# Splitting the last value load and cast of batch 0, making x by halves, and putting a piece of a cast ahead of the weight loads

## The chip, the cores and the metric

The kernel runs on one core of a Trainium2 chip. The metric is the device time of one execution in microseconds (us); less is better. A profile's own clock counts from the first instruction of the program to the last. That length is called the span and is 1.9 to 2.2 us shorter than the device time in the profiled runs here. Engines: PE is the matmul engine, PEld its weight loads, DVE the vector engine, ACT the scalar engine, POOL is GpSimd, SP issues most DMAs.

## The reference

Efficient attention for 8 batches of 8 heads (576 positions, head width 64), then a SwiGLU block over all 4608 tokens:

```python
q_s = softmax(q, axis=-1); k_s = softmax(k, axis=2)          # per head
kv  = einsum('bhsd,bhse->bhde', k_s, v)
x   = einsum('bhsd,bhde->bhse', q_s, kv)                     # tokens x 512
out = (silu(x @ w_gate) * (x @ w_val)) @ w_out               # 512 -> 1536 -> 512
```

## The kernel before

The eight heads make two groups of four, G = 0 and 1. A group's x needs its q (exp, row sums, multiply to `qs`, transpose to `qt`), its k (exp) and its v (cast to bf16). `kv` is K^T V with a column of ones beside V, whose result scales `kv` to `kn`. The block then runs in chunks of tokens: batch 0 is the first chunk (576 tokens). All is issued in a fixed order per engine. The parts that the change touches:

```python
WARM = (64, 8, 8)                         # dummy matmuls, to bring PE to its full clock
def load(b, G, what, src, after=None):    # one DMA on SP's queue, 576 KB
    raw[what, b, G] = ld.tile([128, 2, T * 64], FP32, ...)
    ...
def x(b, G, piece, eng=nc.scalar):        # four 64x64 matmuls side by side
    xp = [f_tile("xp") for _ in range(2)]
    for g in range(2):
        for h in range(2):
            r = slice(64 * h, 64 * h + 64)
            matmul(out=xp[h][64*g:64*g+64, ...], lhsT=kn[r, g, :], rhs=qt[g][r, t0:t1, :])
    ...                                   # xp[0] copied by ACT, xp[1] by DVE
# ---- the start
load q(0,0), q(0,1); for G in 0, 1: load k(0,G), v(0,G)
exp q, norms: qs of group 0 on POOL, of group 1 on DVE
exp(0, 0, "k"); cast_v(0, 0, nc.scalar)
# weights on POOL's queue, fp32 in HBM, cast to bf16 by the DMA, held back until v(0,0) landed
for c0, n in ((0, 256), (256, 256), (512, 512), (1024, 512)): wg slice, wv slice
wo slices (three)
warm_up(WARM[0]); transposes; exp k(0,1); kv(0,0); kn
cast_v(0, 1, nc.vector, *A); cast_v(0, 1, nc.scalar, *Z)     # tiles 0-4 and 5-8
warm_up(WARM[1]); x(0,0,A); x(0,0,Z); kv(0,1); kn
warm_up(WARM[2]); x(0,1,A); x(0,1,Z)
load(1, 0, "q", q, after=w_dma[-3])       # batch 1: after the first wo slice has landed
...
for m in range(12): m_unit(0, S, m)       # g_ps, u_ps: gate and value matmuls of chunk 1
```

The softmax here doesn't subtract the row's maximum and nothing guards it: scores larger than these inputs give would overflow.

Of the kernel before, what the change touches and what calls it, by code (L numbers as in the profile page):

```python
# [8 lines left out]
FP32 = mybir.dt.float32  # L9
# [6 lines left out]
def kernel(  # L16
# [19 lines left out]
    nc = tc.nc  # L36

    B, H, S, D = q.shape
# [4 lines left out]
    T = S // 64  # L43
    HSTR = S * D
    NG = H // 4
    RING = 1536
    WARM = (64, 8, 8)

    const = ctx.enter_context(tc.tile_pool(name="const", bufs=1))
    ld = ctx.enter_context(tc.tile_pool(name="ld", bufs=3))  # L50
# [5 lines left out]
    def f_tile(name):  # L56
        return psp.tile([128, 512], FP32, tag="ps", name=name)
# [4 lines left out]
    xt = const.tile([128, KT, n_tok], BF16, name="xt", tag="xt")  # L62
# [4 lines left out]
    dmas = {}  # L67
    raw = {}

    def load(b, G, what, src, after=None):  # L70
        raw[what, b, G] = ld.tile([128, 2, T * 64], FP32, tag=what, name=what)
        ap = bass.AP(
            tensor=src.tensor,
            offset=src[b, 4 * G].offset,
            ap=[[T * 64, 128], [2 * HSTR, 2], [1, T * 64]],
        )
        d = nc.sync.dma_start(out=raw[what, b, G], in_=ap)  # L77
        if after is not None:
            tc.add_manual_dep(d.ins, after.ins.name, SYNC, reason="order of loads")
        dmas[what, b, G] = d  # L80
# [21 lines left out]
    def copy(eng, out, in_):  # L102
        if eng is nc.scalar:
            nc.scalar.copy(out=out, in_=in_)  # L104
        else:
            eng.tensor_copy(out=out, in_=in_)  # L106


    st = {}
    BANKS = ((0, 5), (5, 9))  # L110

    def exp(b, G, what):
        s = st.setdefault((b, G), {"vb": vbs[G]})
# [7 lines left out]
    def cast_v(b, G, eng, t0=0, t1=T):  # L121
        copy(
            eng,
            vbs[G][:, t0:t1, 0:128].rearrange("p t (h d) -> p t h d", d=64),
            raw["v", b, G].rearrange("p h (t d) -> p t h d", d=64)[:, t0:t1],
        )
# [19 lines left out]
    def norm(b, G):  # L146
        norm_sum(b, G)
        norm_mul(b, G, nc.vector)
# [46 lines left out]
        for g in (1, 0):  # L195
            nc.vector.reciprocal(out=s["kvr"][:, g:g + 1], in_=s["kv"][g][:, 128:129])

    def kn(b, G, g, eng):
        s = st[b, G]
        if "kn" not in s:  # L200
            s["kn"] = at.tile([128, 2, 64], BF16, tag="kn", name="kn")
        for h in range(2):
            r = slice(64 * h, 64 * h + 64)
            out_, src, sc = s["kn"][r, g, :], s["kv"][g][r, r], s["kvr"][r, g:g + 1]
            if eng is nc.scalar:
                nc.scalar.mul(out_, src, sc)
            else:
                nc.vector.tensor_scalar_mul(out_, src, sc)  # L208

    def x(b, G, piece, eng=nc.scalar):  # L210
        s = st[b, G]
        t0, t1 = piece
        n = 64 * (t1 - t0)
# [4 lines that stand above are left out]
                nc.tensor.matmul(  # L218
                    out=xp[h][64 * g:64 * g + 64, 0:n].rearrange("p (t c) -> p t c", c=64),
                    lhsT=s["kn"][r, g, :],  # L220
                    rhs=s["qt"][g][r, t0:t1, :],
                    start=True, stop=True,
                )
        c0 = b * S + 64 * t0
        copy(eng, xt[:, 2 * G, c0:c0 + n], xp[0][:, 0:n])
        nc.vector.tensor_copy(out=xt[:, 2 * G + 1, c0:c0 + n], in_=xp[1][:, 0:n])  # L226

    def x_both(b, G, eng=nc.scalar):
        for piece in BANKS:
            x(b, G, piece, eng)  # L230
        st.pop((b, G))
# [92 lines left out]


    make_identity(nc, ident)
    A, Z = BANKS
    with tc.manual_schedule():
        for G in range(NG):
            load(0, G, "q", q)  # L330
        for G in range(NG):
            load(0, G, "k", k)
            load(0, G, "v", v)
        warm = const.tile([128, 1], FP32, name="warm", tag="warm")
        nc.vector.memset(warm, 0.0)
        nc.scalar.activation(out=warm, in_=warm, func=AF.Exp)
        zero = const.tile([128, 256], BF16, name="zero", tag="zero")
        nc.vector.memset(zero, 0.0)  # L338
        for vb in vbs:
            nc.vector.memset(vb[:, :, 128:129], 1.0)  # L340

        exp(0, 0, "q")
        exp(0, 1, "q")
        norm_sum(0, 0)
        norm_mul(0, 0, nc.gpsimd)
        norm_sum(0, 1)
        norm_mul(0, 1, nc.vector)
        exp(0, 0, "k")
        cast_v(0, 0, nc.scalar)

        w_dma = []
        for c0, n in ((0, 256), (256, 256), (512, 512), (1024, 512)):
            w_dma.append(w_slice(wg, moe_w_gate, c0, n))
            w_dma.append(w_slice(wv, moe_w_val, c0, n))
        tc.add_manual_dep(w_dma[0].ins, dmas["v", 0, 0].ins.name, SYNC, reason="order of loads")
        for m0 in (0, 4, 8):
            w_dma.append(wo_slice(m0, 4))

        warm_up(WARM[0])
        for G in range(NG):  # L360
            for piece in BANKS:
                tr(0, G, piece, nc.vector)
        exp(0, 1, "k")
        kv(0, 0)
        kn_recip(0, 0)
        kn(0, 0, 1, nc.scalar)
        kn(0, 0, 0, nc.vector)
        cast_v(0, 1, nc.vector, *A)
        cast_v(0, 1, nc.scalar, *Z)
        warm_up(WARM[1])  # L370
        x(0, 0, A)
        x(0, 0, Z)
        kv(0, 1)
        kn_recip(0, 1)
        kn(0, 1, 1, nc.scalar)
        kn(0, 1, 0, nc.vector)
        warm_up(WARM[2])
        x(0, 1, A)
        x(0, 1, Z)

        load(1, 0, "q", q, after=w_dma[-3])
        load(1, 1, "q", q)
        for G in range(NG):
            load(1, G, "k", k)
            load(1, G, "v", v)
        load_group(2, 0)

        for m in range(MT):
            m_unit(0, S, m)

        exp(1, 0, "q")
        exp(1, 1, "q")
        exp(1, 0, "k")
        cast_v(1, 0, nc.gpsimd)
        cast_v(1, 1, nc.gpsimd)
        load_group(2, 1)
        o_unit(0, nc.scalar)
        norm(1, 0)
        o_unit(1, nc.scalar)
        exp(1, 1, "k")  # L400
        norm(1, 1)
        o_unit(2, nc.scalar)
        for piece in BANKS:
            tr(1, 0, piece, nc.vector)
        kv_kn(1, 0, split=True)
        for piece in BANKS:
            tr(1, 1, piece, nc.vector)
        exp(2, 0, "q")

        def between():  # L410
            kv_kn(1, 1, split=True)
            x_both(1, 0, nc.vector)

        finish = o_unit(3, between=between)
        exp(2, 0, "k")
        x_both(1, 1)
        finish()
        norm(2, 0)
        tr_dma(2, 0)
        cast_v(2, 0, nc.gpsimd)  # L420
        cast_v(2, 1, nc.gpsimd)
        exp(2, 1, "q")
        exp(2, 1, "k")

        chunks = [(S, 448)] + [(c, 512) for c in range(1024, n_tok, 512)]
        for ci, (c0, n) in enumerate(chunks):
            b = ci + 2
            first_o = 4 * ci
            final = ci == len(chunks) - 1
            steps = {}  # L430
            if ci == 0:
                steps = {2: lambda: kv_kn(2, 0, True), 4: lambda: x_both(2, 0),
                         7: lambda: kv_kn(2, 1, True), 10: lambda: x_both(2, 1)}
            elif b < B:
                steps = {8: lambda: kv_pair(b), 9: lambda: x_both(b, 0),
                         10: lambda: x_both(b, 1)}
            for m in range(MT):
                if ci == 0 and m == 4:
                    norm_sum(2, 1)
                    norm_mul(2, 1, nc.gpsimd)  # L440
                    tr_dma(2, 1)
                    load_group(3, 0)
                    load_group(3, 1)
                if ci > 0 and m in (3, 7):
                    if b < B:
                        att_head(b, m // 4)
                        if m == 7 and b + 1 < B:
                            load_group(b + 1, 0)
                            load_group(b + 1, 1)
                    o_unit(first_o + (0 if m == 3 else 2))  # L450
                    if not (final and m == 7):
                        o_unit(first_o + (1 if m == 3 else 3))
                m_unit(c0, n, m)
                if m in steps:
                    steps[m]()
        o_unit(first_o + 3)
        last = n_tok // 128 - 4
        for j in range(last, last + 3):
            o_unit(j)
        o_last(last + 3)  # L460
# [30 lines left out]
```

## Time and profile before

Median 319.42 us of the first three runs.

| what | at, us | view |
|---|---|---|
| first v of batch 0 lands, weights begin to be issued | 9.68, 9.99 | timeline, DMA landings |
| second v lands | 12.64 | DMA landings |
| first block matmul (g_ps) | 15.68 | timeline of PE |
| third wv load lands, PE waits 0.33 for it | 24.77 | waits of PEld |
| q of batch 1 issued, lands | 33.23, 40.04 | chain of waits |
| second chunk's first matmul | 53.55 | timeline of PE |

The page first: busy time by engine, then (of its picture in 40 slices, 7.9 us each) the tenths in which PE and the DMA engines are busy.

```profile
PE 310.4 (98%) x1920; PEld 157.1 (50%) x1948; DVE 175.5 (55%) x332; ACT 149.2 (47%) x224; POOL 31.1 (10%) x33
...
PE   8999999999999999999999999999999999999995
...
DMA  7999999449145905392519440963150213020134
```

PE is nearly never idle, but in the first six or seven slices the DMA engines are full too. So two resources run abreast at the start. The timeline of POOL before the change (start us, length us, then engine, line, operation, out<-in and, in brackets, idle time before and what ended it):

```profile
7.29 2.12 POOL L140 TENSOR_TENSOR qs<-eq,rr 128x1152 bf16<-128x1152 bf16 x1 [5.99 <-DVE rr L135]
9.99 0.93 POOL L92 DMA_DIRECT2D wg<-in_moe_w_gate_dram  x1 [0.57 <-DMA v<-in_v_dram]
```

The weights start when v has landed. The chain of work that ended last, in order of time, cut to the start of the kernel:

```profile
2.26 7.42 DMA v<-in_v_dram
9.99 0.93 POOL wg L92
16.05 17.16 DMA wo<-in_moe_w_out_dram
33.23 6.82 DMA q<-in_q_dram
40.11 1.28 ACT L115
```

Read it as: v, then the issue of the weights, then a wo load (issued at 16.05, landed at 33.21, behind all weights ahead of it), then q of batch 1, then ACT. In this execution the chain doesn't go through the x of batch 0 at all. PE's timeline and its waits for weights:

```profile
15.26 0.49 PE L218 MATMUL xp<-qt,kn 64*64 64x320 bf16 x8
15.68 1.26 PE L270 MATMUL g_ps<-xt,wg 128*128 128x320 bf16 x8
```
```profile
PEld L270 <- DMA wv<-in_moe_w_val_dram: 0.3, 1, 0.3
```

DVE around the casts:

```profile
9.37 1.36 DVE L140 TENSOR_TENSOR qs<-eq,rr 128x1152 bf16<-128x1152 bf16 x1
...
13.03 0.56 DVE L106 CAST vb<-v 128x640 bf16<-128x640 f32 x1
```
```profile
313.87 0.29 DVE L322 COPY o_sb<-o_ps 128x128 f32<-128x128 f32 x1 [0.38 <-PE o_ps L318]
```

Last, two casts of the same shape on POOL, later in the kernel, of which the first was started during a qs multiply on DVE (44.35 to 45.71):

```profile
44.68 2.03 POOL L106 CAST vb<-v 128x1152 bf16<-128x1152 f32 x1 [25.26 <-ACT ek L115]
...
52.20 1.15 POOL L106 CAST vb<-v 128x1152 bf16<-128x1152 f32 x1 [2.52 <-DMA v<-in_v_dram]
```

### The profile page before, as it was taken

What the parts mean: (1) busy time and instruction counts of PE and PEld (TensorE: products, weight loads), DVE (VectorE), ACT (ScalarE), POOL (GpSimd) and SP (SyncE); (2) the same over time, 40 slices, a digit from 0 to 9 for tenths busy, and PEclk for the clock granted to TensorE, in tenths of its full rate; (3) what the DMA queues carried; (4) which work ended last, traced back from release to release, by engine and by line L of the source; (5) the groups of instructions that cost most, each with busy time, mean ns of one, the idle gap of its engine ahead of it and who ended that gap; (6) DMA issues with size and microseconds to landing.
All of it is one profiled execution on the core that took longest, in us unless ns stands there. A gap on an engine that the chain in (4) does not pass through costs nothing.

```text
span 317.4 us, 5037 instructions
## 1 busy us (share of the span) xinstructions
PE 310.4 (98%) x1920; PEld 157.1 (50%) x1948; DVE 175.5 (55%) x332; ACT 149.2 (47%) x224; POOL 31.1 (10%) x33
## 2 busy tenths in 40 slices
PE   8999999999999999999999999999999999999995
PEld 6777744554445444444444444444444444444444
DVE  2934479964647664774577366746575333333422
ACT  4753387744763475547364547355734122312300
POOL 1930023121100110011001100020000000000000
PEclk9999999999999999999999999999999999999999
DMA  7999999449145905392519440963150213020134
GB/s 269 252 190 206 281 392 393 130 116 367 22 84 153 379 24 103 74 385 94 103 38 355 162 103 1 310 241 64 41 103 2 44 22 67 3 61 5 35 67 99
DMA packets 39176, 46.34 MB, mean 146 GB/s; under 512 B 16368, under 2 KB 22384, under 8 KB 39152
## 3 DMA queue, kind: packets, MB, share of 16 engines
q1 hardware_dynamic: 33104, 41.17, 42.5%
q0 software_dynamic: 5808, 4.72, 9.7%
q8 instruction: 15, 0.25, 0.3%
q10 hardware_dynamic: 240, 0.13, 0.2%
q14 instruction: 9, 0.07, 0.1%
HBM read 37.75 MB, written 9.44 MB: 149 GB/s over the span
## 4 chain that ended last, share of the span: by engine, by line
PE 82%; DMA 10%; DVE 3%; POOL 2%; ACT 1%; issue 1%; SPq 0%; DVEq 0%; ACTq 0%
PE g_ps L270 26%; PE o_ps L297 26%; PE u_ps L270 26%; DMA wo<-in_moe_w_out_dram 5%; PE kv L184 2%; DMA v<-in_v_dram 2%; DMA q<-in_q_dram 2%; PE xp L218 1%; POOL wg L92 1%; POOL wv L92 1%; DVE qs L140 1%; PE o_ps L318 1%; DVE rs L131 1%; DVE xt L226 0%; SPq L77 0%
## 5 line engine op out<-in xcount | busy, mean ns | idle before, releaser
L278 ACT ACTIVATE sg<-g_ps 128x512 bf16<-128x512 f32 (+2 forms) x120 | 64.9, 554 | 132.9 <-PE g_ps L270 126.8
L279 DVE TENSOR_TENSOR hr<-sg,u_ps 128x512 bf16<-128x512 bf16 (+2 forms) x120 | 74.9, 633 | 90.7 <-PE u_ps L270 84.1
L270 PE MATMUL g_ps<-xt,wg 128*128 128x512 bf16 (+2 forms) x469 | 110.3, 358 | 0.7
L270 PE MATMUL u_ps<-xt,wv 128*128 128x512 bf16 (+2 forms) x468 | 109.6, 357 | 0.7
L297 PE MATMUL o_ps<-wo,hr 128*128 128x512 bf16 x415 | 93.3, 379 | 0.3
L270 PEld LDWEIGHTS <-wv 128*128 128x128 bf16 x480 | 46.9, 98 | 46.9 <-issue 0.3
L270 PEld LDWEIGHTS <-wg 128*128 128x128 bf16 x480 | 45.3, 98 | 46.2 <-issue 2.6
L297 PEld LDWEIGHTS <-hr 128*128 128x128 bf16 x420 | 41.0, 98 | 49.1 <-issue 0.2
L106 POOL CAST vb<-v 128x1152 bf16<-128x1152 f32 x14 | 17.8, 1270 | 167.2 <-DMA v<-in_v_dram 115.0
L131 DVE TENSOR_REDUCE rs<-eq 128x18 f32<-128x1152 bf16 x16 | 21.6, 1352 | 21.9 <-ACT eq L115 21.8
L106 DVE COPY o_sb<-o_ps 128x512 f32<-128x512 f32 x32 | 21.1, 686 | 20.6 <-PE o_ps L297 20.6
L140 DVE TENSOR_TENSOR qs<-eq,rr 128x1152 bf16<-128x1152 bf16 x14 | 19.8, 1415 | 0.5
L115 ACT ACTIVATE eq<-q 128x1152 bf16<-128x1152 f32 x16 | 18.5, 1163 | 3.2 <-DMA q<-in_q_dram 3.1
L115 ACT ACTIVATE ek<-k 128x1152 bf16<-128x1152 f32 x16 | 18.4, 1152 | 1.3 <-DMA k<-in_k_dram 1.3
L278 ACT ACT_TABLE_LOAD x12 | 15.4, 1283 | 0.2
L208 DVE TENSOR_SCALAR kn<-kv,kvr 64x64 bf16<-64x64 f32 x52 | 14.7, 283 | 1.3
L115 ACT ACT_TABLE_LOAD x11 | 14.1, 1283 | 0.9 <-DMA q<-in_q_dram 0.7
L104 ACT CAST xt<-xp 128x320 bf16<-128x320 f32 (+1 forms) x30 | 10.5, 402 | 6.6 <-PE xp L218 6.6
L226 DVE CAST xt<-xp 128x320 bf16<-128x320 f32 (+1 forms) x32 | 13.1, 450 | 0.5 <-PE xp L218 0.5
L249 PE MATMUL warm_ps<-zero 128*128 128x256 bf16 x80 | 10.9, 302 | 1.1 <-DVE zero L338 1.1
L184 PE MATMUL kv<-vb,ek 64*128 64x129 bf16 x288 | 10.3, 218 | 0.2 <-DVE vb L106 0.2
L184 PEld LDWEIGHTS <-ek 64*128 64x128 bf16 x288 | 8.4, 94 | 3.9 <-ACT sg L278 2.1
(32 smaller groups left out, 64.5 us busy)
## 6 DMA issues: line engine op xcount, KB each, us to landing
q<-in_q_dram SPq DMA_DIRECT2D x16, 576.0 KB, 7.0
k<-in_k_dram SPq DMA_DIRECT2D x16, 576.0 KB, 8.5
v<-in_v_dram SPq DMA_DIRECT2D x16, 576.0 KB, 9.4
out_dram<-o_sb SPq DMA_DIRECT2D x70, 128.0 KB, 2.4
wo<-in_moe_w_out_dram POOLq DMA_DIRECT2D x3, 512.0 KB, 19.0
wg<-in_moe_w_gate_dram POOLq DMA_DIRECT2D x2, 512.0 KB, 11.3
wv<-in_moe_w_val_dram POOLq DMA_DIRECT2D x2, 512.0 KB, 13.1
wg<-in_moe_w_gate_dram POOLq DMA_DIRECT2D x2, 256.0 KB, 6.0
```

The costliest lines, as they stand in the source:

```text
L106: eng.tensor_copy(out=out, in_=in_)
L115: nc.scalar.activation(out=s["e" + what], in_=raw[what, b, G].rearrange("p h (t d) -> p t h d", d=64), func=AF.Exp,)
L131: nc.vector.reduce_sum(out=rs, in_=s["eq"].rearrange("p t h d -> p (t h) d"), axis=mybir.AxisListType.X)
L140: eng.tensor_mul(s["qs"].rearrange("p t (h d) -> p (t h) d", d=64), s["eq"].rearrange("p t h d -> p (t h) d"), s["rr"].to_broadcast([128, ...
L184: nc.tensor.matmul(out=s["kv"][g][:, 0:129], lhsT=s["ek"][r, t, :, :].rearrange("p h d -> p (h d)"), rhs=s["vb"][r, t, 0:129], start=(t == 0),
L208: nc.vector.tensor_scalar_mul(out_, src, sc)
L226: nc.vector.tensor_copy(out=xt[:, 2 * G + 1, c0:c0 + n], in_=xp[1][:, 0:n])
L249: nc.tensor.matmul(out=ps[:, 0:256], lhsT=zero[:, 0:128], rhs=zero, start=True, stop=True)
L270: nc.tensor.matmul(out=p_[:, 0:w_], lhsT=w[:, kk, ms], rhs=xt[:, kk, c:c + w_], start=(kk == 0), stop=(kk == KT - 1),)
L278: nc.scalar.activation(out=sg[:, 0:w_], in_=g_ps[:, 0:w_], func=AF.Silu)
L279: nc.vector.tensor_mul(hr[:, m, r:r + w_], sg[:, 0:w_], u_ps[:, 0:w_])
L297: nc.tensor.matmul(out=o_ps, lhsT=hr[:, m, r0:r0 + 128], rhs=wo[:, m, :], start=(m == 0), stop=(m == MT - 1),)
```

## The change

Its intent is to have the second x of batch 0 sooner, so that the first chunk starts sooner: the second v in two loads, its cast in three pieces, kn and x by half (h = 0, then h = 1) so that the first half's matmuls need only half of kn, fewer dummies in between. A small piece of the first v's cast goes to POOL, and so the weights are issued a little later and leave the queue to the second v.

```diff
-    WARM = (64, 8, 8)
+    WARM = (64, 6, 5)
...
-        for G in range(NG):
-            load(0, G, "k", k)
-            load(0, G, "v", v)
+        load(0, 0, "k", k)
+        load(0, 0, "v", v)
+        load(0, 1, "k", k)
+        load(0, 1, "v", v, None, *A)          # tiles 0-4
+        load(0, 1, "v", v, None, *Z)          # tiles 5-8
...
-        cast_v(0, 0, nc.scalar)
+        cast_v(0, 0, nc.scalar, 0, 7)
+        cast_v(0, 0, nc.gpsimd, 7, 9)         # POOL, ahead of the weights' issue
...
         cast_v(0, 1, nc.vector, *A)
-        cast_v(0, 1, nc.scalar, *Z)
+        cast_v(0, 1, nc.scalar, 5, 7)
+        cast_v(0, 1, nc.vector, 7, 9)
...
-        kn(0, 1, 1, nc.scalar)
-        kn(0, 1, 0, nc.vector)
+        for h in range(2):
+            kn(0, 1, 1, nc.scalar, h, h + 1)
+            kn(0, 1, 0, nc.vector, h, h + 1)
         warm_up(WARM[2])
-        x(0, 1, A)
-        x(0, 1, Z)
+        x_by_half(0, 1)                       # per h, per piece: two matmuls (g = 0, 1), one copy
```

More of the change, by code (lines that the diff above doesn't have):

```diff
@@ L68, with load @@
     raw = {}
-    def load(b, G, what, src, after=None):
-        raw[what, b, G] = ld.tile([128, 2, T * 64], FP32, tag=what, name=what)
+    def load(b, G, what, src, after=None, t0=0, t1=T):
+        if (what, b, G) not in raw:
+            raw[what, b, G] = ld.tile([128, 2, T * 64], FP32, tag=what, name=what)
         ap = bass.AP(
             tensor=src.tensor,
-            offset=src[b, 4 * G].offset,
-            ap=[[T * 64, 128], [2 * HSTR, 2], [1, T * 64]],
+            offset=src[b, 4 * G].offset + 64 * t0,
+            ap=[[T * 64, 128], [2 * HSTR, 2], [1, (t1 - t0) * 64]],
         )
-        d = nc.sync.dma_start(out=raw[what, b, G], in_=ap)
+        d = nc.sync.dma_start(out=raw[what, b, G][:, :, t0 * 64:t1 * 64], in_=ap)
         if after is not None:
@@ L109 @@
     st = {}
-    BANKS = ((0, 5), (5, 9))
+    A, Z = BANKS = ((0, 5), (5, 9))
     def exp(b, G, what):
@@ L196, in kn_recip, with kn @@
             nc.vector.reciprocal(out=s["kvr"][:, g:g + 1], in_=s["kv"][g][:, 128:129])
-    def kn(b, G, g, eng):
+    def kn(b, G, g, eng, h0=0, h1=2):
         s = st[b, G]
@@ L201, in kn @@
             s["kn"] = at.tile([128, 2, 64], BF16, tag="kn", name="kn")
-        for h in range(2):
+        for h in range(h0, h1):
             r = slice(64 * h, 64 * h + 64)
@@ L226, in x, with x_by_half @@
         nc.vector.tensor_copy(out=xt[:, 2 * G + 1, c0:c0 + n], in_=xp[1][:, 0:n])
+    def x_by_half(b, G):
+        s = st[b, G]
+        for h, eng in ((0, nc.scalar), (1, nc.vector)):
+            r = slice(64 * h, 64 * h + 64)
+            for t0, t1 in BANKS:
+                n = 64 * (t1 - t0)
+                xp = f_tile("xp")
+                for g in range(2):
+                    nc.tensor.matmul(
+                        out=xp[64 * g:64 * g + 64, 0:n].rearrange("p (t c) -> p t c", c=64),
+                        lhsT=s["kn"][r, g, :],
+                        rhs=s["qt"][g][r, t0:t1, :],
+                        start=True, stop=True,
+                    )
+                c0 = b * S + 64 * t0
+                copy(eng, xt[:, 2 * G + h, c0:c0 + n], xp[:, 0:n])
     def x_both(b, G, eng=nc.scalar):
@@ L326 @@
     make_identity(nc, ident)
-    A, Z = BANKS
     with tc.manual_schedule():
```

## The prediction

> **What bounds the kernel.** The page: PE busy 98% of 317.4 us, so only idle or dummy PE time can be won. The timeline: real FFN matmuls begin at 15.68 us and then have almost no gap. The front is bound by a second thing, the DMA queues, full from 2.5 to 47.5 us (the page's DMA digits). Landings in the trace: first v of batch 0 at 9.68, second v 12.64; then the weights in order of issue: wg 15.18, wv 16.37, 18.39, 19.69, wg 22.22, wv 24.77, 28.18, 30.66, wo 33.21. Only then is q of batch 1 issued; it lands at 40.04, just when ACT wants it. PE already waits for this chain: the fifth u_ps group starts at 24.81 after 0.33 us for a wv load; and the chain of waits runs wo load, q load, table load, exp, two norms on DVE, transposes at 48.73, x, g_ps at 54.6.
>
> So x(0,1) being ready earlier gains nothing alone: PE would wait longer at 24.8 and 48.7. What counts is when the weights land.
>
> **What the change does.**
> 1. x by half: the first pair of kn (0.3 us each) releases the first matmuls, about 0.3 us less before x. But DVE gets one more cast, of 128x256 (estimate 0.25 us, from 0.56 for 128x640), ahead of its xt copies. Together about 0. The second v landed at 12.64 but its casts began at 13.01, behind kn, so landing earlier is hardly used.
> 2. Five dummy matmuls fewer: 5 x 0.12 us, not on the chain.
> 3. A 128x256 cast on POOL goes ahead of the weights' issue (before: 9.99). DVE's qs multiply runs 9.37 to 10.73. The Trainium skill, "SBUF — State Buffer", section "Who interferes with whom", says that a DVE instruction with two SBUF inputs and a GpSimd one that reads SBUF block each other for a whole instruction. The trace agrees: a POOL cast alone took 1.15 us (at 52.2), but 2.03 and 1.99 when started during a qs multiply, ending 1.00 after it both times. So the cast should wait to 10.73 and end near 10.95 (2/9 of 1.0), and the first weight issue move to about 11.0. The queue was partly filled with v until 12.1, so I estimate that weights land about 0.5 us later (82 KB moved before the new start, at 160 GB/s). If the cast isn't blocked, 0.1 to 0.2.
>
> **Sum.** x about where it was (15.3), g_ps 15.7 to 15.9, perhaps a short new wait for the first wv; the fifth u_ps group starts near 25.3; q of batch 1 lands near 40.5; all the rest shifts by 0.3 to 0.5 us. Nothing else changes after 55 us, nor the PE clock.
>
> Predicted: 319.7 us, 8 in 10 between 318.7 and 320.7. Faster by over 2%: 0.005; within 2%: 0.985; slower by over 2%: 0.01.
>
> **What would show it.** POOL's small cast ends after DVE's qs multiply; first wg issue near 11.0; third wv landing after 25.0; a longer wait of u_ps on wv; q of batch 1 later than 40.1. Wrong if the first wg issue comes before 10.4, or the weights land no later.
>
> **What would make it wrong.** The weights, no longer sharing the queue with v, may land as early as before; then the time is the same to 0.2 us. Or fewer bubbles in their stream (110 GB/s at 15 to 16 us, otherwise 160) give up to 0.5 us of gain. Fewer dummies could drop the PE clock; I don't expect it.

## More of the kernel before

```profile
SPq L486 <- DMA out_dram<-o_sb: 0.7, 3, 0.3
```

The end of the kernel (last copy of the result; who SP waited for after it): from the end of that last copy (314.17) to the end of the span (317.37) there are 3.20 us. I call this stretch the tail; the prediction did not look at it.

## The result, and the profile after

The changed kernel took 320.8 us (median of six runs, 319.96 to 321.56), beside 319.35. The ratio is 1.0044 with a 95% interval of 1.0023 to 1.0065. Ratios here are the mean time of one kernel's fast runs over that of the other's of the same rounds, so not quite the ratio of the medians. In two later jobs of six runs each the changed kernel had 1.0021 and 1.0035. It is slower by 0.2 to 0.45%, about 1.06 us on average (means of 1.39, 0.72 and 1.08 us). The forecast was 0.3 us, with 320.7 us as the upper end of its range.

The profile of the changed kernel. POOL, whose cast now stands between qs and the weights:

```profile
7.31 2.12 POOL L141 TENSOR_TENSOR qs<-eq,rr 128x1152 bf16<-128x1152 bf16 x1 [6.00 <-DVE rr L136]
9.41 1.49 POOL L107 CAST vb<-v 128x256 bf16<-128x256 f32 x1
10.85 0.93 POOL L93 DMA_DIRECT2D wg<-in_moe_w_gate_dram  x1
```

DVE: its qs multiply, and its two casts of the second v in one row:

```profile
8.70 1.94 DVE L141 TENSOR_TENSOR qs<-eq,rr 128x1152 bf16<-128x1152 bf16 x1
...
12.95 1.16 DVE L107 CAST vb<-v 128x640 bf16<-128x640 f32 x2
```

The multiply ended at 10.64 and the POOL cast 0.25 us after it, so a cast of 256 columns took 1.49 us. PE, and its waits:

```profile
15.47 0.75 PE L237 MATMUL xp<-qt,kn 64*64 64x320 bf16 x8 [0.36 <-DVE kn L209]
16.15 1.15 PE L288 MATMUL g_ps<-xt,wg 128*128 128x320 bf16 x8
...
26.69 1.15 PE L288 MATMUL u_ps<-xt,wv 128*128 128x320 bf16 x8 [0.98 <-DMA wv<-in_moe_w_val_dram]
```
```profile
PEld L288 <- DMA wv<-in_moe_w_val_dram: 1.8, 2, 1.3
```

The wait for the third wv grew from 0.33 to about a microsecond on PE. The chain of waits after, again cut to its start:

```profile
7.31 2.12 POOL qs L141
9.43 1.47 POOL vb L107
10.90 0.88 POOL wg L93
14.70 11.94 DMA wv<-in_moe_w_val_dram
26.69 1.15 PE u_ps L288 x8
```

The small POOL cast, the issues of weights and the third wv load are now the chain, and from 26.69 on it stays with PE; q of batch 1 is no longer on it. And the end of the kernel:

```profile
315.53 0.29 DVE L340 COPY o_sb<-o_ps 128x128 f32<-128x128 f32 x1 [0.38 <-PE o_ps L336]
```
```profile
SPq L507 <- DMA out_dram<-o_sb: 1.3, 1, 1.3
```

Here the tail (315.82 to 319.44) is 3.62 us, and SP's waits for the stores look different: one of 1.3 us in place of three of at most 0.3.

A DMA is done when all of its 16 shares, one from each DMA engine, have landed. The times of the 16 for the third wv load, read from its semaphore's updates in the two traces:

```
before  23.39 23.89 23.96 24.12 24.13 24.19 24.20 24.21 24.26 24.29 24.35 24.36 24.44 24.47 24.63 24.77
after   24.09 24.11 24.14 24.26 24.33 24.34 24.36 24.38 24.41 24.45 24.46 24.55 24.61 24.81 25.68 26.64
```

The middle of the load is 0.2 us later than before, the last share 1.9 us. This agrees with what the Trainium skill, "DMA: Bandwidth & Descriptors", section "Why a DMA increments its semaphore by 16 and not by 1", says: the engines finish independently, and only the full count means that all has landed. The forecast reckoned with a load as a whole.

### The profile page after: what moved, and what is told of

Read it like the earlier page. It is cut to its first block, busy times and chain, and to the rows that moved or that the text cites. A ratio compares the mean times of both kernels' runs of the same rounds, so it can differ in the third digit from the quotient of the medians.

```text
span 319.4 us, 5059 instructions
## 1 busy us (share of the span) xinstructions
PE 312.2 (98%) x1943; PEld 156.6 (49%) x1943; DVE 175.7 (55%) x333; ACT 149.1 (47%) x224; POOL 33.0 (10%) x34
## 4 chain that ended last, share of the span: by engine, by line
PE 89%; DMA 5%; POOL 2%; DVE 2%; ACT 0%; issue 0%; POOLq 0%
PE g_ps L288 28%; PE u_ps L288 28%; PE o_ps L315 28%; DMA wv<-in_moe_w_val_dram 4%; PE kv L185 3%; PE xp L219 1%; DMA q<-in_q_dram 1%; PE o_ps L336 1%; POOL wg L93 1%; POOL qs L141 1%; POOL wv L93 0%; POOL vb L107 0%; DVE xt L227 0%; DVE rs L132 0%; ACT eq L116 0%; PE tp L161 0%
## 5 line engine op out<-in xcount | busy, mean ns | idle before, releaser
L288 PE MATMUL u_ps<-xt,wv 128*128 128x512 bf16 (+2 forms) x480 | 111.0, 358 | 1.2 <-DMA wv<-in_moe_w_val_dram 1.2
L288 PE MATMUL g_ps<-xt,wg 128*128 128x512 bf16 (+2 forms) x480 | 111.6, 358 | 0.2
L107 POOL CAST vb<-v 128x1152 bf16<-128x1152 f32 (+1 forms) x15 | 19.8, 1317 | 166.7 <-DMA v<-in_v_dram 114.5
L227 DVE CAST xt<-xp 128x320 bf16<-128x320 f32 (+1 forms) x30 | 12.2, 448 | 0.0
```

What stands on the lines that cost most here:

```text
L107: eng.tensor_copy(out=out, in_=in_)
L227: nc.vector.tensor_copy(out=xt[:, 2 * G + 1, c0:c0 + n], in_=xp[1][:, 0:n])
L288: nc.tensor.matmul(out=p_[:, 0:w_], lhsT=w[:, kk, ms], rhs=xt[:, kk, c:c + w_], start=(kk == 0), stop=(kk == KT - 1),)
```

## The experiments

There were five jobs; within a job all kernels share one chip and the runs of the kernel before. The names: a_ is the changed kernel with something taken back, b_ is the kernel before with one thing done. All results were correct; one execution was slow, and is told of. What the traces showed, in us; the last columns are explained below the table:

| kernel | ratio (95% interval) | first wg issued | third wv landed | q of batch 1 landed | first g_ps | chunk 2 begins | tail |
|---|---|---|---|---|---|---|---|
| before | 1 | 9.99 | 24.77 | 40.04 | 15.68 | 53.55 | 3.20 |
| after | 1.0044 (1.0023, 1.0065) | 10.85 | 26.64 | 41.19 | 16.15 | 55.21 | 3.62 |
| after_again | 1.0021 (1.0006, 1.0036) | 10.94 | 24.51 | 39.94 | 16.25 | 53.59 | 3.62 |
| after_third | 1.0035 (1.0020, 1.0049) | 10.94 | 25.98 | 40.53 | 16.26 | 54.55 | 3.64 |
| a_nopool | 1.0006 (0.9993, 1.0018) | 10.23 | 24.63 | 39.55 | 17.04 | 54.44 | 3.65 |
| b_pool | 1.0009 (0.9998, 1.0021) | 10.87 | 25.40 | 40.70 | 16.51 | 54.20 | 3.19 |
| b_pool_again | 1.0014 (0.9998, 1.0029) | 11.05 | 25.84 | 40.83 | 16.68 | 54.42 | 3.21 |
| b_split | 1.0010 (0.9996, 1.0023) | 10.37 | 25.25 | 40.73 | 16.75 | 54.24 | 3.63 |
| b_tiny1 | 1.0005 (0.9993, 1.0018) | 9.52 | 24.19 | 38.93 | 15.90 | 53.36 | 3.62 |
| a_tiny7 | 1.0025 (1.0012, 1.0039) | 10.93 | 26.09 | 40.47 | 16.25 | 54.66 | 3.20 |
| b_warm54 | 1.0002 (0.9990, 1.0015) | 10.11 | 25.25 | 39.79 | 15.74 | 53.82 | 3.19 |
| b_qearly | 1.0021 (1.0006, 1.0036) | 10.53 | 25.47 | 37.96 | 16.16 | 55.33 | 3.22 |
| b_delay2 | 1.0075 (1.0046, 1.0104) | 12.01 | 26.69 | 41.10 | 16.14 | 57.00 | 3.19 |
| b_xhalf | 1.0004 (0.9991, 1.0017) | 10.36 | 25.30 | 39.63 | 15.99 | 53.86 | 3.20 |
| b_early | 1.0003 (0.9989, 1.0016) | 9.58 | 25.47 | 40.58 | 15.95 | 54.08 | 3.21 |
| best2 | 0.9991 (0.9977, 1.0005) | 9.48 | 24.30 | 39.34 | 15.85 | 53.30 | 3.23 |
| best2_again | 0.9994 (0.9978, 1.0009) | 9.41 | 24.10 | 38.52 | 15.93 | 53.77 | 3.20 |
| a_fix (fast runs) | 0.9989 (0.9976, 1.0003) | slow | slow | slow | slow | slow | slow |
| a_fix_again | 1.0002 (0.9990, 1.0014) | 9.43 | 24.36 | 38.67 | 16.23 | 53.58 | 3.19 |
| best3 | 1.0007 (0.9992, 1.0021) | 9.37 | 24.30 | 38.81 | 16.18 | 54.26 | 3.21 |

"Chunk 2 begins" is the first matmul of the second chunk. Between it and the end of the last copy of the result there are 260.6 to 260.7 us in every fast trace: span = beginning of chunk 2 + 260.6 + tail. So all that the change can do is in two numbers, and the rest of the kernel is a constant. One trace is one execution, and executions of one kernel differ by several tenths; the ratios rest on five or six runs (eleven of before in the later jobs).

### Is the late share a matter of chance? (after_again, after_third: no edit)

> The changed kernel once more, unchanged. In its first trace 14 of the 16 shares of the third wv load had landed by 24.8 us, but the last two at 25.7 and 26.6, and PE waited 0.98 us for the last. Theory S (a late share is a matter of chance in each execution): the late shares are elsewhere or smaller in this trace, the wait of u_ps on the third wv is under 0.6 us, and the time of this execution is near 320. Theory P (it belongs to the change): again two late shares, third wv whole after 26 us. Time: 1.003 to 1.006 of before.

> The changed kernel unchanged, for the size of its loss: 1.002 to 1.0045. Weights issued at 10.9 us once more, third wv whole between 24.5 and 26.7 us, tail 3.6 us.

In after_again the third wv was whole at 24.51 and its last two shares 0.01 us apart; PE did not wait for it. In after_third the last share came 0.75 us after the one before, and PE waited 0.78 us. So the size of the lag is different in each execution. It is not the change's alone either: in b_early (below) one share came 1.5 us after the other fifteen. What makes a DMA engine fall behind stays open; the packed traces don't say which engine a share came from. The issue of the weights, however, was at 10.85 to 10.94 in all four traces with the whole change's POOL piece (a_tiny7 is the fourth).

after_again shows one thing more. The chain of waits that ended last has no load of weights or of batch 1 there. It goes through DVE's casts of the second v and x of batch 0 (at 15.56) to the first g_ps; two of its lines:

```profile
13.33 0.87 DVE vb L107 x2
16.32 1.09 PE g_ps L288 x8
```

Chunk 2 begins 37.34 us after the first g_ps there (16.25 to 53.59), with no wait of PE over 0.25 us between. In nine of the 19 fast traces the chain goes through x in this way: after_again, a_nopool, b_pool_again, b_split, b_tiny1, best2, best2_again, a_fix_again and best3. In the other ten it comes from a late load. So there are two limits, and the later one counts.

### One part taken out, or done alone (a_nopool, b_pool, b_pool_again, b_split)

a_nopool, out of the changed kernel, and b_pool the reverse, into the kernel before:

```diff
-        cast_v(0, 0, nc.scalar, 0, 7)
-        cast_v(0, 0, nc.gpsimd, 7, 9)
+        cast_v(0, 0, nc.scalar)
```

b_split is the kernel before with the second v in two loads, as in the change's diff, and nothing else.

> The changed kernel with the first v cast whole on ACT, as before, so that the weights are issued right after v lands. Theory 1 (the POOL piece, held up by the qs multiply, delays the weights, and all else follows): first weight issue back at about 9.9 us, third wv whole by 25.0, time within 0.1% of before (ratio 0.999 to 1.001). Theory 2 (the split load of the second v, with its smaller packets, or the DVE casts, make the weights late): still 1.003 or more. Theory 3 (x comes later): g_ps still starts near 16.1 us, and the time is 1.001 to 1.002.

> The kernel before with one part of the change alone: the last two ninths of the first v cast on POOL ahead of the weights' issue. Theory 1: cast ends right after the qs multiply, first weight issue at 10.8 us, third wv later than 25 us, ratio 1.003 to 1.005, all of the change's loss. Theories 2 and 3: ratio under 1.002.

> The kernel before with the second v of batch 0 in two loads and nothing else. Theory 1: ratio 0.999 to 1.001. Theory 2 (the two loads leave some of the 16 DMA engines behind, and the weights behind them): late shares of the weights, ratio 1.002 or more.

> The kernel before with the POOL piece alone, once more: first weight issue at 10.9 us, tail 3.2 us, ratio 1.0005 to 1.002; about the changed kernel's ratio less 0.0013 for the tail.

POOL in b_pool, and in a_nopool:

```profile
9.70 1.22 POOL L106 CAST vb<-v 128x256 bf16<-128x256 f32 x1 [0.25 <-DMA v<-in_v_dram]
10.87 0.93 POOL L92 DMA_DIRECT2D wg<-in_moe_w_gate_dram  x1
```
```profile
10.23 0.94 POOL L93 DMA_DIRECT2D wg<-in_moe_w_gate_dram  x1 [0.71 <-DMA v<-in_v_dram]
```

DVE's multiply ended at 10.66 in b_pool, the cast at 10.92: held up again. But neither single part had the whole loss, as my theory 1 wanted. b_pool's mean was 0.36 and 0.47 us over before, a_nopool's 0.36, b_split's 0.36. All four intervals hold 1, so the sizes are rough; a_nopool against the changed kernel in the same job is 0.37 us less. The trace of a_nopool has its own delay: PE's full clock came late (6.98 us), g_ps began at 17.04, and chunk 2 began 37.4 us after that. Theory 1 alone falls: something else is in a_nopool and in b_split, and the traces say where. Their tail is 3.65 and 3.63 us, as in all traces with the split load, and 3.2 in all without.

### The tail (b_tiny1, a_tiny7)

DMAs of SP and ACT take eight semaphores (the counters by which a DMA tells that it has landed) in turn. At the end of the program SP waits for each semaphore, one after the other, in a fixed order. The second v in two loads is one DMA more, so from there on every DMA has the next semaphore. SP's last waits, by the time each was over, read from the traces, with the landing of the last store:

```
before  315.22 315.29 315.36 315.42 315.48 315.64 315.86 316.23 316.52                    last store lands 316.47
after   316.86 318.16 318.23 318.29 318.35 318.41 318.47 318.53 318.59                    last store lands 318.12
```

Before, the last store had the semaphore that is waited for last, so the other waits were done by the time it landed. After, it has one that is waited for second: SP stands there until 318.12, and only then goes through the seven others, at about 0.06 us each. That is the 0.42 us. To test it, small DMAs that nobody reads, in the middle of the kernel (one into the kernel before, seven into the changed kernel):

```diff
+                if ci == 3 and m == 9:
+                    scr = const.tile([128, 8], FP32, name="scr", tag="scr")
+                    for e in range(1):        # a_tiny7: range(7)
+                        nc.sync.dma_start(out=scr[:, e:e + 1], in_=<one column of q>)
                 m_unit(c0, n, m)
```

> The kernel before with one further DMA of 512 bytes in the middle (about 150 us), read by nobody. Theory T (tail): in four traces with the second v in two loads, the time from the last copy of the result to the end is 0.41 us longer than in the two traces without, because the count of DMAs on the eight semaphores shifts by one, the last store falls on the semaphore that SP waits for second to first at the end, and seven waits of about 0.06 us follow it instead of one. So this kernel too has a tail 0.4 us longer (3.6 us from the last copy's end to the end of the span, not 3.2), and a ratio near 1.0013. If the tail comes of the split load itself, the tail is as before.

> The changed kernel with seven such DMAs of 512 bytes in the middle, so that the count is 8 more than before and the last store has its old semaphore again. Theory T: the tail is back to 3.2 us, and the time is 0.4 us below the changed kernel's: ratio 1.0005 to 1.001 where the changed kernel had 1.002. Rival: the tail stays at 3.6 us, and the ratio at 1.002 or more.

The ends of b_tiny1 (span 317.6) and of a_tiny7 (span 318.5), last copy and SP's waits:

```profile
313.67 0.29 DVE L322 COPY o_sb<-o_ps 128x128 f32<-128x128 f32 x1 [0.38 <-PE o_ps L318]
```
```profile
SPq L494 <- DMA out_dram<-o_sb: 1.2, 1, 1.2
```
```profile
314.99 0.29 DVE L340 COPY o_sb<-o_ps 128x128 f32<-128x128 f32 x1 [0.38 <-PE o_ps L336]
```
```profile
SPq L515 <- DMA out_dram<-o_sb: 0.8, 3, 0.3
```

One DMA of 512 bytes, at 172.8 us in this trace, makes the tail 3.62 us, and seven bring the changed kernel's back to 3.20. The cause of the longer tail is settled: it is the place of the last store among the eight semaphores (one DMA more than before, or eight more), not the split load as such. The times are not as clear: b_tiny1 had 1.0005, not 1.0013, and a_tiny7 1.0025, no less than after_again in another job. Its trace shows why: the third wv landed at 26.09 and PE waited 0.65 us for it. The spread of the loads hides 0.4 us in six runs; the tail in the traces does not vary by more than 0.05.

### Do the landings hang on the issue? (b_delay2)

```diff
+        pad = const.tile([128, 2304], FP32, name="pad", tag="pad")
+        d = nc.gpsimd.memset(pad, 0.0)        # waits for v(0,0), ahead of the weights
```

> The kernel before with a memset of an unused 128x2304 tile on POOL ahead of the weights' issue, waiting for the same v [...]. Theory D (loads of the weights hang on their issue one to one, and the time on their landing): first weight issue near 12 us, third wv lands near 26.8 us, q of batch 1 near 42 us, PE waits over 1 us for the third wv, ratio 1.005 to 1.007. If the landings are set by the queue and not by the issue, they move by under 1 us and the ratio stays under 1.003.

The issue moved by 2.02 us (9.99 to 12.01) and the third wv by 1.92 (24.77 to 26.69), but q of batch 1 only by 1.06 (40.04 to 41.10, not to 42). One trace is little to go by. A straight line through the 20 traces (one of them slow) gives 0.89 us of landing of the third wv for each us of issue (standard error 0.15), and 0.86 for q of batch 1 (0.23). So landings follow the issue nearly one to one on average. The time grew by 2.4 us on average, but not by the landings alone. What I hadn't foreseen is in PE's timeline and in the busy time of stretches of this trace (columns: stretch, length, busy us and count of PE, PEld, DVE, ACT, POOL, granted PE clock, DMA share, GB/s):

```profile
18.97 2.10 PE L270 MATMUL u_ps<-xt,wv 128*128 128x320 bf16 x8 [1.68 <-DMA wv<-in_moe_w_val_dram]
20.87 1.91 PE L270 MATMUL g_ps<-xt,wg 128*128 128x320 bf16 x8
22.61 1.14 PE L270 MATMUL u_ps<-xt,wv 128*128 128x320 bf16 x8
```
```profile
15.00:19.00 4.00, 2.01 (x21) 1.04 (x20) 1.13 (x4) 3.00 (x6) 4.00 (x6) 1.00 1.36 178
19.00:22.40 3.40, 3.40 (x15) 2.15 (x16) 0.82 (x2) 0.00 (x0) 1.51 (x3) 0.50 1.29 197
```

After an idle time of 1.68 us PE's clock was halved for 3.4 us, and eight matmuls took 2.10 us, not 1.14. Three of the six runs had a mean clock of 0.992 to 0.995 and took 322.8 to 323.5 us; the three with 0.999 to 1.0 took 320.5 to 321.4, which is 1.3 us over before on average. So at full clock the 2.0 us of delay cost 1.3 us, and the runs with the lower clock took another 2.2: waiting for a load can be paid twice. In the changed kernel the clock didn't fall so (0.997 to 1.0).

### x by half (b_xhalf)

> The kernel before with x of the second group by half, kn by head, and three dummy matmuls fewer just before it; no split load, no new cast. In the traces of the changed kernel x begins about 0.3 us after the first kn, but its eight matmuls then take 0.69 us to the first g_ps rather than 0.42, since a half has only two matmuls that run side by side where the old form has four. Theory X: x begins 0.2 to 0.3 us sooner and g_ps no sooner than before (15.6 to 15.9 us after an early clock), ratio 0.9995 to 1.0005. The intent of the change would give g_ps 0.3 us sooner.

In the kernel before with kn and x by half (with WARM (64, 8, 5)), x and the first g_ps began as follows:

```profile
15.30 0.76 PE L236 MATMUL xp<-qt,kn 64*64 64x320 bf16 x8
15.99 1.15 PE L287 MATMUL g_ps<-xt,wg 128*128 128x320 bf16 x8
```

From x to g_ps there are 0.69 us, where before there were 0.42. The old form starts four 64x64 matmuls within 0.06 us of each other, on four quarters of the array (in the trace of before at 15.257, 15.312, 15.316 and 15.319); by half it is two at a time, and four such pairs take their turns. x itself began at 15.30, before at 15.26, but in this execution the second v had landed 0.37 us later (13.01, before 12.64), and kn began 0.31 us later (14.90, before 14.59). Against kn, then, x began 0.27 us sooner, as expected. What the halved kn wins, x by half gives back. The ratio 1.0004 fits.

### Attempts at a faster kernel (b_warm54, b_qearly, b_early, best2, best2_again)

b_warm54 has WARM = (54, 8, 8); b_qearly has `after=w_dma[-4]` for the loads of batch 1; b_early holds the weights back for the first k in place of the first v; best2 and best2_again are b_early with WARM = (54, 8, 8).

> The kernel before with 54 dummy matmuls at the start, not 64. The traces show that PE gets its full clock between 4.1 and 6.8 us, differently in each execution, and that the 64 dummies then end between 9.6 and 10.9 us, in four of six traces after the qs that the transposes wait for. Theory W (this start is the spread of the times, and costs on average 0.3 us): dummies end by 9.8 us in every execution, g_ps starts by 15.8, and the ratio is 0.998 to 0.9995. Rival (the loads bound the start anyway, or the idle PE loses its clock): 1.000 or more.

> The kernel before with the loads of batch 1 let go one weight load earlier (after the last wv, not the first wo). Theory D (the time is the later of two chains: g_ps of the first chunk plus 37.35 us on PE, and landing of q of batch 1 plus 13.5 us; before, the second ended it): q lands near 37.5 us rather than 40.0, the wait goes over to PE, and the ratio is 0.998 to 0.9995. Rival: the last wo load, needed at 41 us, becomes late, and the ratio is 1.000 or more.

> The kernel before with the weights held back by the first k of batch 0 and not by the first v, so that POOL issues them as soon as its qs is done, at 9.45 us and no longer at v's landing (9.5 to 10.5 in six traces). The opposite of what the change does. Theory D: third wv by 24.2 us, q of batch 1 by 39.4, ratio 0.998 to 0.9995. Rival: the weights take bandwidth from the second v, x comes later, ratio 1.000 or more.

> The same with 54 dummy matmuls at the start, so that neither a late clock nor a late v moves the start. Theories D and W together: g_ps by 15.8 us, q by 39.4, ratio 0.998 to 0.999, with a smaller spread than before. Rival: as before.

> The kernel before with weights let go by the first k and 54 dummies, once more: 0.9985 to 0.9995, and a smaller spread than before. If the first result was chance: 1.000.

The 64 dummies at the start, in the traces of before and of b_split, an identical piece of program:

```profile
1.09 8.81 PE L249 MATMUL warm_ps<-zero 128*128 128x256 bf16 x64 [1.09 <-DVE zero L338]
```
```profile
1.09 10.09 PE L250 MATMUL warm_ps<-zero 128*128 128x256 bf16 x64 [1.09 <-DVE zero L341]
```

PE got its full clock after 14 to 28 dummies, between 4.2 and 7.1 us in the fast traces, so the same 64 end up to 1.3 us apart. In b_split the transposes had to wait until 11.02 (9.74 and 10.79 in before), and its g_ps began at 16.75. That is one source of the spread between executions, and a reason to be wary of the column "first g_ps" in the table. With 54 dummies g_ps began at 15.7 to 15.9 (b_warm54, best2, best2_again) though the clock came as late as 6.7, and the clock held. The ratio of b_warm54 is 1.0002 all the same; in its trace the third wv (25.25) is on the chain, and not x.

b_qearly shows what else is close behind: q landed 2 us sooner as forecast, but wo paid for it.

```profile
43.25 2.97 PE L297 MATMUL o_ps<-wo,hr 128*128 128x512 bf16 x13 [1.05 <-DMA wo<-in_moe_w_out_dram]
```

The rival had it right: the ratio is 1.0021. b_early alone won nothing (1.0003; in its trace one share was 1.5 us late). best2 was ahead by 0.31 and 0.22 us in two jobs, but both intervals hold 1: not shown to be faster.

### Are the late weights and the tail the whole of it? (a_fix, a_fix_again, best3)

a_fix is the changed kernel with both taken out: the cast whole on ACT as in a_nopool, and the seven small DMAs of a_tiny7. The split load, the cast in pieces, x by half and the fewer dummies stay. best3 adds the early weights and 54 dummies.

> The changed kernel without its POOL piece (first v cast whole on ACT, weights issued at v's landing) and with the seven small DMAs that bring the last store back to its old semaphore. If the late weights and the longer tail are the whole of the loss: third wv by 25.3 us, tail 3.2 us, ratio 0.9995 to 1.0008. If there is a third cause (x by half, the DVE casts, the split load): 1.001 or more.

> The same as a_fix: the changed kernel without its POOL piece and with the seven small DMAs. If late weights and the longer tail are the whole of the loss: tail 3.2 us, third wv by 25.3 us, ratio 0.9985 to 1.0005. Where the first result was chance: 1.001 or more.

> a_fix with the weights let go by the first k of batch 0, and 54 dummies at the start. If the gains add up: third wv by 24.5 us, q of batch 1 by 39.4 us, ratio 0.998 to 0.9995, spread under 0.3 us. If PE or x now bounds the start: as a_fix.

The profiled execution of a_fix was a slow one of 546 us, at a mean clock of 0.559: PE was granted 0.56 of its clock from 4.8 us on and never all of it. It is left out. The five fast runs had 0.9989, those of a_fix_again 1.0002. In the job of a_fix the changed kernel unchanged had 1.0035, so taking the two out took back 1.5 us there (means). No third cause of a loss is needed, and the rest of the change is no gain that these runs could show. The trace of a_fix_again shows why there is none: q of batch 1 landed at 38.67, but g_ps began only at 16.23, and chunk 2 37.35 us after it (53.58, before 53.55). best3, at 1.0007, shows no sum of the two lines of attempts: in its trace PE waited 0.67 us at 49.4 for transposes' input, a wait that I did not follow further.

## Why the prediction was wrong

- **What bounds the kernel**: half right. With the weights or q of batch 1 late, chunk 2 is late, and all after it is constant (260.6 us). But "x(0,1) being ready earlier gains nothing" holds only while a load is the later limit, as in the traces of before and after. In nine of the 19 fast traces x and the first g_ps were.
- **The POOL cast is held up by DVE's multiply, weights issued near 11.0**: right. The cast ended 0.25 to 0.26 us after the multiply in all six traces with the POOL piece, and the issue was at 10.85 to 10.94. The lock told of in the Trainium skill, "SBUF — State Buffer", section "Who interferes with whom", agrees in both directions: in the trace after, DVE's multiply was itself stretched to 1.94 us (1.36 before), as it started (8.70) while POOL's qs ran until 9.43.
- **"Weights land about 0.5 us later"**: this term, for the landing, was mis-sized. It came from the view that the queue had been partly filled with v, so that only part of the 1 us counts. Over the four traces with the whole change's POOL piece the third wv landed at 25.8 on average, over the nine (one of them slow) with the weights at v's landing at 25.0: 0.85 us, for an issue 0.82 us later (10.92 and 10.10). The line through all traces gives 0.89 us for each us. What it cost in time is less sure: b_pool was 0.36 and 0.47 us over before, which lies within the forecast 0.3 to 0.5. In the execution on record the middle of the third wv was only 0.2 us later, and two late shares made it 1.9.
- **The step that failed for certain, a term missing from the sum**: "Nothing else changes after 55 us" was wrong. The runs show the tail in its place, 0.42 us longer. The order of instructions that I had compared did show every DMA's semaphore shifted by one; I took it for a change of names.
- **x about where it was**: off by about 0.4 us. g_ps began at 16.15 to 16.26, not 15.7 to 15.9. The small DVE cast took 0.40 to 0.55 us in the four traces, not the 0.25 estimated; in the trace on record kn began 0.48 us later than before (15.07 and 14.59). The halved kn wins 0.27 us and x by half gives it back on PE. So the second x, which the change was to have sooner, came later. It had no effect in the execution on record, where the third wv came later still, but it set the beginning of chunk 2 in after_again. Nor are the dummies never on the chain: in five of the nine traces above, all with 8 dummies before x, the chain goes through these.
- **The clock**: right, it did not fall with fewer dummies.
- **The sum**: 0.42 of tail and 0.4 to 0.8 of the rest (0.42 is the mean of the b_pool runs, the weights alone; 0.78 is what a_tiny7, without the tail, is over before, late weights and late x together) make 0.8 to 1.2 us, where 1.06 is the mean over 18 runs. The tail's part is settled; the rest is rough, and how much of it is the later x is not shown. That the first six runs had 1.4 us is within what their spread (0.6 us) allows.

## What to carry to other kernels

Look for what the chain of waits goes through before making something else faster; here a step that was not on it in the trace was to be sped up at the price of a delay of one that was. And look at more than one execution: where two limits are within a microsecond, the chain changes from one to the other. One more DMA isn't free even where it is hidden: it may shift which semaphore the last store has, and the waits at the end then come after it, not before. When a cast is put on POOL ahead of DMA issues, look at what DVE runs at that time, since the issues inherit the wait.

## What the Trainium skill lacked or had wrong

- "TensorE: Matmul & The Clock Gate", Part 1, says that the clock's turn comes around 4 us into matmul activity, ±0.5 us from run to run. In the fast traces here it came 3.1 to 6.0 us after the first matmul (14 to 28 dummies of 128x256), a range of 3 us, and this moved the end of 64 dummies by up to 1.3 us.
- The same section gives the drop to half clock as following an idle window of about 3.4 us. In b_delay2 it came after a gap of 1.68 us, PE having been busy 2.01 of the 4.0 us before; it lasted 3.4 us, as the window there says. One execution of a_fix was granted 0.56 of the clock to its end (546 us in place of 319).
- No page that I read has the waits at the end of a program: one semaphore after the other in a fixed order, 0.06 us each, so that the last store's place in it is worth 0.42 us.
- "DMA: Bandwidth & Descriptors" says that the 16 engines finish independently, and that two of them are usually slower, but not how far apart they land. Here the last share of the third wv load (512 KB) came from 0.01 to 1.5 us after the one before it, in different executions, and the lag stayed about the same in the following loads (last wv 0.95, first wo 0.91 us in the trace after). Which engine it was is not recorded.
